# Pack attention and SwiGLU on one core: where the score products of later attentions stand in the matmul order

## The chip, the cores and the metric

The kernel runs on one core of a Trainium2 chip. TensorE multiplies (its matmuls are the rows PE, its weight loads PEld), VectorE (DVE) and ScalarE (ACT) work on what it leaves in PSUM, GpSimd (POOL) and SyncE (SP) do memsets and transfers. The metric is the device time of one execution in microseconds; the median of three runs before is 758.79 us.

## What is computed

Eight batches, each with eight heads, 576 tokens and 64 dimensions, go through two attentions, and the result goes through a gated feed-forward network:

```python
def _attn_ref(q, k, v, p):
    p_packed = sm_attn(p, k, v)              # 32 packed queries against 576 keys
    return sm_attn(q, p_packed, p_packed)    # 576 queries against the 32 packed rows

def _moe_ref(x, w_gate, w_val, w_out):       # x: 4608 x 512, d_ff 1536
    g = x @ w_gate
    silu = g * (1.0 / (1.0 + np.exp(-g)))
    val = x @ w_val
    return silu * val @ w_out
```

## The kernel before

**One batch at a time.** The kernel never forms the attention's output. For each batch b it multiplies the packed rows with the gate and value weights (the product M), and the attention weights a2 of the second attention then multiply M. M and a2 are split into a high and a low part (mh and ml, a2h and a2l), and three products of the parts stand for one in full precision.

**The steady loop.** Batches 1 to 7 run through a loop over twelve chunks fc of 128 hidden columns. In each chunk PE makes gate and value of the first 256 tokens ("A", 12 matmuls of 256 columns, `gv_chunk` with is_b False), then the output products of the previous chunk's A part (6 matmuls of 512 columns, `outs`, `out_mm`), then gate and value of the remaining 320 tokens ("B", 12 matmuls of 320 columns), then the output products of the previous chunk's B part. Chunk 0 has no output products, since there is no previous chunk: A of chunk 0, B of chunk 0 and A of chunk 1 follow each other without a gap. In the odd chunks M of the next pair of chunks follows A (`m_part`, 8 tiled matmuls of 512 columns on 64x32 tiles); in chunk 11 it is the first M of the next batch. After odd batches the leftover tokens of two batches follow as one more block of output products (p4) before the next batch starts.

**PSUM.** There are eight banks: four accumulators (acc), two for gate and value (gv), two for everything else (aux). A uses both gv banks, and so does B: gate goes to the first, value to the second. ACT reads the first (silu into sg), DVE multiplies the second with sg (hf), ACT rounds hf to hh, and DVE makes hl, the rest. A chunk's gate can start only when ACT has read the previous gate from the first bank, its value only when DVE has read the previous value from the second.

**The attention of the next batch** (d = b + 1) is put between these matmuls. For d of 2 and more its steps are: scores of the packed queries (`q_scores`, two groups of 16 tiled matmuls of 144 columns, each followed on DVE by two maxima and two subtractions, L335 and L336), exponentials on ACT, sums, a gather through DRAM of maxima and sums, the factors, a scaling and a transposing of the weights, the packing product (`q_pack`, L395, 80 small matmuls of 32 columns), and its transpose ppt. Then come the scores of the second attention (`s2_mm`, two blocks of 8 tiled matmuls of 288 columns, moved to SBUF by transposes, L421), maximum, exponential, sum, scale (L459), transpose back (L468) and split.

**What sets the order.** PE follows the program's order as it is written. In the steady loop a generator, `aux_of`, is advanced at the 4th and 8th call of `fill` in chunks 1 to 11, which are the places behind the output products of A and of B. Exponentials on ACT wait in a list, `late`, and the next `gv_chunk` takes one from it directly after its silu (L551). DVE and ACT instructions of the attention are pinned to this order (`pin`); the lows ml of M on DVE (L487, `m_lows`) are issued inside `m_part`. Each change between silu and exp on ACT is an ACT_TABLE_LOAD.

Of the kernel before, what the change touches and what calls it, by code (L numbers as in the profile page):

```python
# [59 lines left out]
def tile_pack_attention_swiglu(ctx: ExitStack, tc: tile.TileContext, qT, kT, v, vq, pT, wgv, wout, out):  # L60
# [30 lines left out]
    def pin(ins):  # L91

        return tc.keep_in_program_order(ins) if steady[0] else ins

    late = []

# [214 lines left out]

    def q_scores(b):


        k_t, p_t = kps[b]
        e = pool.tile([P, NPAR, NHP, NKQ * NP], F32, tag="s2", bufs=1, name="e1")
        z = pool.tile([P, 2, NPAR, NHP], F32, tag="z1", bufs=2, name="z1")
        sq[b] = (e, z)
        nc.gpsimd.memset(e[:, :, :, SQ:], 0.0)
        for g in range(2):  # L320
            pss = [ps(), ps()]
            for i in range(2):
                for j in range(NJ):
                    for par in range(NPAR):
                        r = slice(64 * par, 64 * par + 64)
                        nc.tensor.matmul(  # L326
                            pss[par][NP * j : NP * j + NP, i * SQ : (i + 1) * SQ],
                            p_t[r, 2 * g + i, :],
                            k_t[r, j // 2, 2 * g + i, j % 2 * SQ : j % 2 * SQ + SQ],
                            start=True, stop=True,  # L330
                        )
            hs = slice(2 * g, 2 * g + 2)
            for par in range(NPAR):
                x, m = pss[par][:, : 2 * SQ].rearrange("p (h n) -> p h n", h=2), z[:, 0, par, hs]
                pin(nc.vector.tensor_reduce(m, x, axis=AX.X, op=ALU.max))  # L335
                pin(nc.vector.tensor_tensor(  # L336
                    e[:, par, hs, :SQ], x, m.unsqueeze(2).broadcast_to([P, 2, SQ]), op=ALU.subtract
                ))
            late.append(lambda hs=hs: pin(nc.scalar.activation(e[:, :, hs, :SQ], e[:, :, hs, :SQ], AF.Exp, scale=SCALE)))
            yield  # L340
            if g == 0:
                yield

    def q_weights(b):


        e, z = sq[b]
        for g in range(2):
            if g:
                yield  # L350
            hs = slice(2 * g, 2 * g + 2)
            pin(nc.vector.tensor_reduce(z[:, 1, :, hs], e[:, :, hs, :SQ], axis=AX.X, op=ALU.add))
        zv = z.rearrange("p s r h -> p s (r h)")
        x = pool.tile([P, NJ, 2, H], F32, tag="x1", bufs=1, name="x1")
        zd = dram.tile([P, 2, H], F32, tag="zd", bufs=2, name="zd")
        nc.sync.dma_start(zd, zv)
        for i in range(NJ):
            nc.sync.dma_start(x[NP * i : NP * i + NP], zd.rearrange("(j n) s h -> n j s h", j=NJ))
        for _ in range(2):
            yield  # L360
        y = pool.tile([P, 3, NJ + 1, H], F32, tag="pp", bufs=1, name="y1")
        m, t, f = y[:, 2, 0], y[:, 2, 1], y[:, 2, 2]
# [4 lines left out]
        pin(nc.vector.tensor_tensor(y[:, 0, NJ], zv[:, 0], m, op=ALU.subtract))  # L367
        late.append(lambda: pin(nc.scalar.activation(y[:, 0], y[:, 0], AF.Exp, scale=SCALE)))
        yield
# [5 lines left out]
        yield  # L375
        a1 = pool.tile([P, NPAR, NHP, NKQ, NP], F32, tag="a1", bufs=1, name="a1")
        for par in range(NPAR):
            w = e[:, par, :, :SQ]
            pin(nc.vector.tensor_tensor(
                w, w, f[:, NHP * par : NHP * par + NHP].unsqueeze(2).broadcast_to([P, NHP, SQ]), op=ALU.mult  # L380
            ))
            pin(nc.vector.transpose(
                a1[:, par].rearrange("p h k n -> p (h k n)"), e[:, par].rearrange("p h n -> p (h n)")
            ))
            yield
        sq[b] = a1

    def q_pack(b):
        a1, v_t = sq.pop(b), vs.pop(b)
        p_p = ps()  # L390
        for hp in range(NHP):
            for k in range(NKQ):
                for g in range(P // NP):
                    par, ds = g // 2, slice(g % 2 * NP, g % 2 * NP + NP)
                    nc.tensor.matmul(  # L395
                        p_p[NP * g : NP * g + NP, NP * hp : NP * hp + NP],
                        a1[:, par, hp, k, :], v_t[:, par, hp, k, ds],
                        start=(k == 0), stop=(k == NKQ - 1),
                    )
        ppts[b] = pool.tile([P, P], F32, tag="ppt", bufs=2, name="ppt")  # L400
        pin(nc.vector.transpose(ppts[b], p_p[:, :P]))

# [19 lines left out]

    def s2_scores(b):
        for c in range(2):
            s2_mm(b, c)
            s2_block(b, c)
            yield

# [88 lines left out]
    def m_part(b, k, fcs):  # L517
        m_mm(b, k, fcs)
        m_high(b, k, fcs)
        m_lows()  # L520

# [7 lines left out]

    def gv_chunk(b, fc, is_b, fill):  # L530
        odd = b % 2
# [46 lines left out]

    def aux_of(b):

        d = b + 1
        if d == B:
            return
        yield from q_scores(d)
        yield from q_weights(d)
        if d + 1 < B:
            load_k(d + 1)
        q_pack(d)
        yield
        yield  # L590
        if d < B - 1:
            load_v(d + 1)
        s2_tiles(d)
        yield from s2_scores(d)
        if d < B - 1:
            load_q(d + 1)
        s2_a2(d)
        order = (1, 0) if d % 2 else (0, 1)
        halves = [slice(c, c + 1) for c in order]
        first, second = halves  # L600
        s2_max(d, first)
        late.append(lambda: s2_exp(d, first))
        yield
        s2_sums(d, first)
        yield
        s2_max(d, second)
        late.append(lambda: s2_exp(d, second))
        yield
        s2_scale(d, first)
        low = s2_back(d, first.start)  # L610
        yield
        low()
        s2_sums(d, second)
        yield
        s2_scale(d, second)
        low = s2_back(d, second.start)
        yield
        low()

    with tc.manual_schedule(engines={mybir.EngineType.PE}):  # L620
# [186 lines left out]
        for b in range(1, B):  # L807
            rows, accs = begin(b)
            aux = aux_of(b)
            ha, hb = {}, {}  # L810
# [7 lines left out]
            for fc in range(NFC):  # L818
                count = [0]

                def fill():
                    count[0] += 1
                    if count[0] == 2:
                        if fc == NFC - 1 and b + 1 < B:
                            run_all(aux)
# [6 lines left out]
                    if fc and count[0] in (4, 8):  # L832
                        next(aux, None)
# [4 lines left out]
                hb[fc] = gv_chunk(b, fc, True, fill)  # L838
                if fc:
                    outs(fc - 1, 1, fill)  # L840
            run_all(aux)
            outs(NFC - 1, 0, lambda: None)
# [48 lines left out]
```

## Time and profile before

| | before |
|---|---|
| median of three runs | 758.79 us (757.84 to 760.37) |
| the profiled execution | 760.24 us, of which its span is 758.5 us |
| PE busy | 745.1 us, 98% of the span |
| DVE, ACT busy | 456.6 us and 369.6 us |
| M in the steady loop | L201, 64x512, 736 rows, mean 601 ns, run on several tiles at once |
| packed-score matmuls | L326, 384 rows, mean 289 ns |
| packing product | L395, 960 rows, mean 198 ns |
| table loads on ACT | 1283 ns each |

A matmul in full precision shows as two rows. A row's length is longer than its turn on the array, since the next matmul starts before it has ended; the turn is read from start to start.

### The profile page before, as it was taken

To read this page: it belongs to the slowest core of one execution; us is meant where nothing else is said; L and a number is where in the kernel's file an instruction comes from. 1 tells how busy PE (TensorE), PEld (TensorE's weight loads), DVE (VectorE), ACT (ScalarE), POOL (GpSimd) and SP (SyncE) were. 2 spreads that over 40 slices of the span, in tenths; PEclk is the share of its full clock that TensorE was granted. 3 is DMA by queue.
4 is the path that set the end of the run, shared out by engine and by line. 5 is a ranking of instruction groups with operands and counts; after the bars stand their busy time and mean duration, and the time that the engine had idled before them with its cause. 6 is when DMAs were issued, how large, how long until landed. Compare 5 with 4: busy or idle time off the path is not lost.

```text
span 758.5 us, 15106 instructions
## 1 busy us (share of the span) xinstructions
PE 745.1 (98%) x6280; PEld 590.6 (78%) x6280; DVE 456.6 (60%) x1004; ACT 369.6 (49%) x662; POOL 2.0 (0%) x13
## 2 busy tenths in 40 slices
PE   7999999999999999998999999999999999999998
PEld 5756666787888878787788887878788787888886
DVE  5997977665756547454674556656475554743334
ACT  3777654653626436452443545464272642633331
POOL 0000000000000000000000000000000000000000
PEclk9999999999999999999999999999999999999999
DMA  9686582203011030122201221100101000010001
GB/s 355 242 319 249 207 313 78 67 3 133 1 70 67 4 134 1 56 69 71 64 29 42 69 72 63 43 15 3 71 2 69 2 3 2 1 56 1 1 1 70
DMA packets 20004, 59.15 MB, mean 78 GB/s; under 512 B 5984, under 2 KB 7008, under 8 KB 17376
## 3 DMA queue, kind: packets, MB, share of 16 engines
q1 hardware_dynamic: 19792, 58.12, 21.2%
q8 instruction: 49, 0.80, 0.4%
q14 instruction: 19, 0.16, 0.1%
q10 hardware_dynamic: 144, 0.07, 0.0%
HBM read 48.69 MB, written 9.49 MB: 77 GB/s over the span
## 4 chain that ended last, share of the span: by engine, by line
PE 95%; DVE 2%; ACT 1%; issue 1%; ACTq 0%
PE gv L544 36%; PE acc L564 30%; PE aux L201 8%; PE gv L721 6%; PE acc L747 5%; PE aux L564 4%; PE aux L395 1%; PE aux L326 1%; DVE ml L487 1%; PE acc L625 1%; PE warm_ps L625 1%; ACT mh L513 1%; PE gv_aux L201 0%; PE aux L277 0%; DVE w L133 0%
## 5 line engine op out<-in xcount | busy, mean ns | idle before, releaser
L551 ACT ACTIVATE sg<-gv 128x256 f32<-128x256 f32 (+1 forms) x168 | 68.9, 410 | 179.7 <-PE gv L544 145.4
L544 PE MATMUL gv<-a2h,ml 128*128 128x256 f32 (+1 forms) x672 | 148.4, 302 | 0.7
L544 PE MATMUL gv<-a2h,mh 128*128 128x256 f32 (+1 forms) x672 | 144.7, 297 | 0.4 <-issue 0.4
L544 PE MATMUL gv<-a2l,mh 128*128 128x256 f32 (+1 forms) x672 | 144.4, 296 | 0.0
L556 DVE TENSOR_TENSOR hf<-gv,sg 128x256 f32<-128x256 f32 x168 | 70.7, 421 | 120.6 <-PE gv L544 101.2
L564 PE MATMUL acc<-wo_h,hl 128*128 128x512 f32 x336 | 136.8, 407 | 0.0
L564 PE MATMUL acc<-wo_l,hh 128*128 128x512 f32 x336 | 132.4, 394 | 0.0
L564 PE MATMUL acc<-wo_h,hh 128*128 128x512 f32 x336 | 131.7, 392 | 0.0
L544 PEld LDWEIGHTS gv<-a2h,ml 128*128 128x128 f32 x672 | 113.9, 189 | 21.7 <-issue 7.6
L107 ACT CAST hh<-hf 128x256 fp32r<-128x256 f32 x168 | 67.9, 404 | 120.5 <-DVE hf L556 120.4
L113 DVE TENSOR_TENSOR hl<-hf,hh 128x256 fp32r<-128x256 f32 x168 | 71.0, 423 | 80.3 <-ACT hh L107 79.8
L544 PEld LDWEIGHTS gv<-a2h,mh 128*128 128x128 f32 x672 | 109.0, 191 | 0.6 <-issue 0.6
L544 PEld LDWEIGHTS gv<-a2l,mh 128*128 128x128 f32 x672 | 108.5, 190 | 0.0
L564 PEld LDWEIGHTS acc<-wo_h,hl 128*128 128x128 f32 x336 | 63.4, 189 | 42.5 <-issue 34.4
L564 PEld LDWEIGHTS acc<-wo_h,hh 128*128 128x128 f32 x336 | 63.3, 188 | 14.6
L564 PEld LDWEIGHTS acc<-wo_l,hh 128*128 128x128 f32 x336 | 63.4, 189 | 7.7
L487 DVE TENSOR_TENSOR ml<-aux,mh 128x512 fp32r<-128x512 f32 x92 | 59.0, 683 | 6.4 <-ACT mh L513 6.3
L201 PE MATMUL aux<-w,ppt 64*32 64x512 f32 (+1 forms) x784 | 52.4, 588 | 0.5 <-ACT mh L513 0.5
L513 ACT CAST mh<-aux 128x512 fp32r<-128x512 f32 x92 | 49.2, 588 | 3.6 <-PE aux L201 0.7
L747 PE MATMUL acc<-wo_f,h 128*128 128x512 f32 x96 | 44.2, 594 | 0.0
L551 ACT ACT_TABLE_LOAD x30 | 38.5, 1283 | 4.2 <-issue 3.6
L747 PEld LDWEIGHTS acc<-wo_f,h 128*128 128x128 f32 x96 | 17.3, 189 | 17.2 <-issue 15.7
(145 smaller groups left out, 756.0 us busy)
## 6 DMA issues: line engine op xcount, KB each, us to landing
st<-in_wgv SPq DMA_DIRECT2D x12, 1024.0 KB, 6.9
k_t<-in_kT SPq DMA_DIRECT2D x16, 576.0 KB, 4.9
q_t<-in_qT SPq DMA_DIRECT2D x16, 576.0 KB, 5.0
out<-ot SPq DMA_DIRECT2D x36, 256.0 KB, 2.1
v_t<-in_vq SPq DMA_DIRECT2D x6, 1280.0 KB, 5.7
st<-in_wout SPq DMA_DIRECT2D x6, 1024.0 KB, 7.2
v_t<-in_v SPq DMA_DIRECT2D x2, 1024.0 KB, 8.3
p_t<-in_pT SPq DMA_DIRECT2D x7, 64.0 KB, 2.5
```

Source lines behind the costliest of these rows:

```text
L107: e.copy(dst, src)
L113: lo.tensor_tensor(dst_l, src, dst_h.bitcast(F32), op=ALU.subtract)
L201: nc.tensor.matmul(outs[par][32 * hp : 32 * hp + 32], lhs(r, hp), rhs(r, hp), start=True, stop=True)
L487: nc.vector.tensor_tensor(*lows.pop(0), op=ALU.subtract)
L513: nc.scalar.copy(m[0][at], src)
L544: nc.tensor.matmul(pg[:, :n], m_[:, g, f, s * P : (s + 1) * P], a_[:, g, off : off + n], start=(i == 0), stop=(i == 5),)
L551: nc.scalar.activation(sg[:, :n], pgs[0][:, :n], AF.Silu)
L556: nc.vector.tensor_tensor(hf, pgs[1][:, o : o + 256], sg[:, o : o + 256], op=ALU.mult)
L564: nc.tensor.matmul(acc[:, :], h_[:, c : c + P], w_[fc // 2][:, fc % 2], start=(fc == 0 and i == 0), stop=(fc == NFC - 1 and i == 2),)
L625: nc.tensor.matmul(at[:, :P], ident, ident, start=True, stop=True)
L721: nc.tensor.matmul(held[i][s][:, :n], m_[:, g, f, s * P : (s + 1) * P], a_[:, g, off : off + n], start=(j == 0), stop=(j == len(todo) - 1),)
L747: nc.tensor.matmul(accs[2 * is_b + c], half(i)[:, c * P : c * P + P], wos[fc // 2][:, fc % 2], start=(fc == 0), stop=(fc == NFC - 1),)
```

## The change

The generator is gone. A table, `plan_of(b)`, names for each chunk and place which steps run there. The places are "a" (on ACT directly behind the silu of A), "m" (behind A, and behind M where there is one), 4 and 8 as before, and "b". The first packed scores of d move from chunk 1 of batch d - 1 to the place "m" of chunk 11 of batch d - 2 (for d = 2: to place 4 of chunk 0), the second to "m" of chunk 1, the two blocks of the second attention's scores to "m" of chunks 7 and 9. All of these but the first of d = 2 take the two gv banks in place of the aux banks. The packing product is made in two halves, at places 4 and 8 of chunk 6. The first exponential stands at "a" of chunk 0 (for d = 2 of chunk 1), the others at "a" of chunks 2, 4, 8 and 10. The lows of M are pinned, and are issued behind the steps of place "m".

```diff
-    def q_scores(b):
+    def gv_ps():
+        return ps_gv.tile([P, 512], F32, tag="gv", name="gv_aux")
+
+    def q_scores(b, g, bank=ps):
...
-            pss = [ps(), ps()]
+        pss = [bank(), bank()]
...
-    def q_pack(b):
-        a1, v_t = sq.pop(b), vs.pop(b)
-        p_p = ps()
-        for hp in range(NHP):
+    def q_pack(b, half):
+
+        if half == 0:
+            sq[b].append(ps())
+        a1, p_p = sq[b][4:]
+        v_t = vs[b]
+        for hp in range(2 * half, 2 * half + 2):
...
-    def s2_mm(b, c):
-        two[b, c] = [ps(), ps()]
+    def s2_mm(b, c, bank=ps):
+        two[b, c] = [bank(), bank()]
...
-            nc.vector.tensor_tensor(*lows.pop(0), op=ALU.subtract)
+            pin(nc.vector.tensor_tensor(*lows.pop(0), op=ALU.subtract))
...
-        if late:
-            late.pop(0)()
+        behind()
...
+                at(0, "a", lambda: q_exp(d, 0))
+            at(1, "m", lambda: q_scores(d, 1, gv_ps))
...
+            at(6, 4, lambda: q_pack(d, 0))
+            at(6, 8, lambda: q_pack(d, 1))
...
+            at(8, 8, lambda: s2_sums(d, cs), lambda: s2_scale(d, cs), lambda: s2_turn(d, c), lambda: s2_high(d, c))
+            at(9, "m", lambda: s2_mm(d, c2, gv_ps), lambda: s2_block(d, c2))
...
+            at(10, 8, lambda: s2_sums(d, cs2), lambda: s2_scale(d, cs2), lambda: s2_turn(d, c2))
...
+            at(11, "m", lambda: q_scores(d + 1, 0, gv_ps))
...
-                ha[fc] = gv_chunk(b, fc, False, fill)
+                ha[fc] = gv_chunk(b, fc, False, fill, lambda: run(fc, "a"))
+                run(fc, "m")
+                m_lows()
```

In the rows below, the first operand behind the arrow is the moving data. On PE in chunk 1 of a batch before the change (aux<-w,ppt is M, acc the output products, aux<-k_t,p_t the packed scores, gv with 320 columns is B):

```order
L544 MATMUL gv<-a2h,mh 128x256 x2
L201 MATMUL aux<-w_82,ppt 32x512 x8
L564 MATMUL acc<-wo_h,hl 128x512
L564 MATMUL acc<-wo_l,hh 128x512
L564 MATMUL acc<-wo_h,hh 128x512
L564 MATMUL acc<-wo_h,hl 128x512
L564 MATMUL acc<-wo_l,hh 128x512
L564 MATMUL acc<-wo_h,hh 128x512
L326 MATMUL aux<-k_t,p_t 32x144 x16
L544 MATMUL gv<-a2h,ml 128x320 x2
```

The same place after the change:

```order
L552 MATMUL gv<-a2h,mh 128x256 x2
L199 MATMUL aux<-w_82,ppt 32x512 x8
L328 MATMUL gv_aux<-k_t,p_t 32x144 x16
L571 MATMUL acc<-wo_h,hl 128x512
L571 MATMUL acc<-wo_l,hh 128x512
L571 MATMUL acc<-wo_h,hh 128x512
L571 MATMUL acc<-wo_h,hl 128x512
L571 MATMUL acc<-wo_l,hh 128x512
L571 MATMUL acc<-wo_h,hh 128x512
L552 MATMUL gv<-a2h,ml 128x320 x2
```

The scores have moved ahead of the six output products, directly behind M, and write the gv banks that B needs next.

On ACT at the start of a batch that follows a p4 block, before the change (sg of 256 is the silu of A, sg of 320 that of B, ot the last output copies of the previous batch):

```order
L107 COPY ot<-acc 128x512 x2
L551 ACTIVATE sg<-gv 128x256
L107 CAST hh<-hf 128x256
L551 ACTIVATE sg<-gv 128x320
L107 CAST hh<-hf 128x256
```

And after the change:

```order
L105 COPY ot<-acc 128x512 x2
L559 ACTIVATE sg<-gv 128x256
L344 ACT_TABLE_LOAD
L344 ACTIVATE e_4250<-e_4250 128x2x2x144
L105 CAST hh<-hf 128x256
L559 ACT_TABLE_LOAD
L559 ACTIVATE sg<-gv 128x320
L105 CAST hh<-hf 128x256
```

Between the silu of A and the silu of B in chunk 0 there are now a table load, an exponential and a second table load.

On DVE in chunks 10 and 11 after the change (hf of A11, the end of the second attention's scaling, its transpose back into t_4211, then the packed scores of a later attention, and the lows of M):

```order
L462 TENSOR_REDUCE r_3939<-s_3938 128x18
L563 TENSOR_TENSOR hf<-gv,sg 128x256
L463 TENSOR_SCALAR r_3939<-r_3939 128x18
L464 RECIPROCAL r_3939<-r_3939 128x18
L468 TENSOR_TENSOR s_3938<-s_3938,r_3939 128x576
L111 TENSOR_TENSOR hl<-hf,hh 128x256
L477 STREAM_TRANSPOSE t_4211<-s_3938 128x576
L337 TENSOR_REDUCE z_4251<-gv_aux 128x2
L338 TENSOR_TENSOR e_4250<-gv_aux,z_4251 128x2x144
L496 TENSOR_TENSOR ml<-aux,mh 128x512 x2
```

The reading of the score banks (L337 and L338, each there twice) stands behind the scaling and the transpose; in chunk 9 the two block transposes of the second scores stand at the same place behind the same instructions.

## Rows read from the trace of the kernel before

**Rows 1.** The page: busy time of each engine with its share of the span, and the chain of work that ended last, by engine.

```profile
PE 745.1 (98%) x6280; PEld 590.6 (78%) x6280; DVE 456.6 (60%) x1004; ACT 369.6 (49%) x662; POOL 2.0 (0%) x13
...
PE 95%; DVE 2%; ACT 1%; issue 1%; ACTq 0%
```

**Rows 2.** The timeline of PE in chunk 7 of batch 4 (start and length in us, engine, line, operation, tile, shape, and how many matmuls one row stands for): the end of A, M, the last output products, the two blocks of second-attention scores (L201 with q_t), and what follows each.

```profile
452.08 0.40 PE L544 MATMUL gv<-a2l,mh 128*128 128x256 f32 x2
...
452.32 0.40 PE L544 MATMUL gv<-a2h,mh 128*128 128x256 f32 x2
...
453.67 0.50 PE L564 MATMUL acc<-wo_h,hl 128*128 128x512 f32 x1
...
454.70 0.39 PE L564 MATMUL acc<-wo_l,hh 128*128 128x512 f32 x1
...
454.93 0.40 PE L564 MATMUL acc<-wo_h,hh 128*128 128x512 f32 x1
...
456.43 0.56 PE L544 MATMUL gv<-a2h,ml 128*128 128x320 f32 x2
...
459.45 0.40 PE L564 MATMUL acc<-wo_h,hh 128*128 128x512 f32 x1
...
459.78 0.72 PE L201 MATMUL aux<-q_t,ppt 64*32 64x288 f32 x16
...
460.43 0.50 PE L544 MATMUL gv<-a2h,ml 128*128 128x256 f32 x2
```

**Rows 3.** The waits: engine, line and tile that waited, what released it, us in total, times, longest.

```profile
PEld aux L201 <- DVE ml L487: 4.6, 12, 0.4
PEld aux L326 <- DVE ml L487: 4.6, 12, 0.4
```

**Rows 4.** The timeline of PE around the packing product: the three rows of the one in batch 4, and the last row of the one in batch 3 (the bracket is the idle time before the row).

```profile
446.07 0.39 PE L564 MATMUL acc<-wo_h,hh 128*128 128x512 f32 x1
...
446.38 1.56 PE L395 MATMUL aux<-v_t,a 128*32 128x32 f32 x160
...
447.88 0.56 PE L544 MATMUL gv<-a2h,ml 128*128 128x320 f32 x2
```

```profile
352.64 0.33 PE L395 MATMUL aux<-v_t,a 128*32 128x32 f32 x15 [2.01 <-issue]
```

**Rows 5.** Busy time in the stretch behind that row: length, then busy us of PE, PEld, DVE, ACT and POOL with their instructions, granted clock of PE (1.00 is full), DMA share, GB/s.

```profile
353.00:360.00 7.00, 7.00 (x46) 5.88 (x46) 1.72 (x5) 1.40 (x4) 0.00 (x0) 0.76 0.54 190
```

**Rows 6.** The timeline at the start of batch 4 (behind a p4 block) and of batch 3 (without one): silu of A0, start of A1, M behind A1, and the output copy on ACT.

```profile
405.15 0.38 ACT L551 ACTIVATE sg<-gv 128x256 f32<-128x256 f32 x1 [6.80 <-DVE ot L109]
...
407.45 0.40 PE L544 MATMUL gv<-a2h,ml 128*128 128x256 f32 x2
...
409.30 1.09 PE L201 MATMUL aux<-w,ppt 64*32 64x512 f32 x16
```

```profile
307.97 0.38 ACT L551 ACTIVATE sg<-gv 128x256 f32<-128x256 f32 x1 [1.54 <-PE gv L544]
...
308.66 0.59 ACT L107 COPY ot<-acc 128x512 f32<-128x512 f32 x1 [0.31 <-DMA out<-ot]
...
310.27 0.40 PE L544 MATMUL gv<-a2h,ml 128*128 128x256 f32 x2
...
312.12 1.09 PE L201 MATMUL aux<-w,ppt 64*32 64x512 f32 x16
```

**Rows 7.** The timeline of ACT where it changes to exp and back between two silus, in chunks 9 and 10 of batch 4.

```profile
471.66 0.44 ACT L551 ACTIVATE sg<-gv 128x320 f32<-128x320 f32 x1 [0.68 <-PE gv L544]
472.11 1.28 ACT L446 ACT_TABLE_LOAD   x1
473.41 0.69 ACT L446 ACTIVATE s<-s 128x576 f32<-128x576 f32 x1
474.00 0.39 ACT L107 CAST hh<-hf 128x256 fp32r<-128x256 f32 x1
474.61 1.28 ACT L551 ACT_TABLE_LOAD   x1 [0.23 <-issue]
475.91 0.38 ACT L551 ACTIVATE sg<-gv 128x256 f32<-128x256 f32 x1
```

**Rows 8.** The timeline: DVE's hf of A1 and the first output product behind M in batch 4; DVE in chunks 10 and 11 of that batch (hf, scale, transpose back, hl); the block transposes of chunk 7; a maximum and a subtraction of the packed scores.

```profile
409.48 0.42 DVE L556 TENSOR_TENSOR hf<-gv,sg 128x256 f32<-128x256 f32 x1 [0.43 <-PE gv L544]
...
410.32 0.50 PE L564 MATMUL acc<-wo_h,hl 128*128 128x512 f32 x1
```

```profile
479.04 0.41 DVE L556 TENSOR_TENSOR hf<-gv,sg 128x256 f32<-128x256 f32 x1
...
480.27 0.75 DVE L459 TENSOR_TENSOR s<-s,r 128x576 f32<-128x576 f32 x1
...
481.67 0.77 DVE L468 STREAM_TRANSPOSE t<-s 128x576 f32<-128x576 f32 x1
482.36 0.38 DVE L113 TENSOR_TENSOR hl<-hf,hh 128x256 fp32r<-128x256 f32 x1
```

```profile
460.59 0.85 DVE L421 STREAM_TRANSPOSE s<-aux 128x288 f32<-128x288 f32 x2 [0.70 <-PE aux L201]
```

```profile
413.24 0.46 DVE L335 TENSOR_REDUCE z<-aux 128x2 f32<-128x288 f32 x1 [0.85 <-PE aux L326]
...
413.73 0.46 DVE L336 TENSOR_TENSOR e<-aux,z 128x288 f32<-128x288 f32 x1
```

More of the change, by code (lines that the diff above doesn't have):

```diff
@@ L344, in q_weights @@
-    def q_weights(b):
-        e, z = sq[b]
[L348 to L353, printed above, removed]
+        if g == 0:
+            e = pool.tile([P, NPAR, NHP, NKQ * NP], F32, tag="s2", bufs=1, name="e1")
+            z = pool.tile([P, 2, NPAR, NHP], F32, tag="z1", bufs=2, name="z1")
+            sq[b] = [e, z]
+            nc.gpsimd.memset(e[:, :, :, SQ:], 0.0)
@@ new lines, in q_scores @@
+        e, z = sq[b]
+        pss = [bank(), bank()]
+        for i in range(2):
+            for j in range(NJ):
+                for par in range(NPAR):
+                    r = slice(64 * par, 64 * par + 64)
+                    nc.tensor.matmul(
+                        pss[par][NP * j : NP * j + NP, i * SQ : (i + 1) * SQ],
+                        p_t[r, 2 * g + i, :],
+                        k_t[r, j // 2, 2 * g + i, j % 2 * SQ : j % 2 * SQ + SQ],
+                        start=True, stop=True,
+                    )
@@ new lines, in q_scores, with q_exp @@
+        hs = slice(2 * g, 2 * g + 2)
+        for par in range(NPAR):
+            x, m = pss[par][:, : 2 * SQ].rearrange("p (h n) -> p h n", h=2), z[:, 0, par, hs]
+            pin(nc.vector.tensor_reduce(m, x, axis=AX.X, op=ALU.max))
+            pin(nc.vector.tensor_tensor(
+                e[:, par, hs, :SQ], x, m.unsqueeze(2).broadcast_to([P, 2, SQ]), op=ALU.subtract
+            ))
+    def q_exp(b, g):
+        x = sq[b][0][:, :, 2 * g : 2 * g + 2, :SQ]
+        pin(nc.scalar.activation(x, x, AF.Exp, scale=SCALE))
@@ L374, in q_weights, with q_turn @@
         pin(nc.vector.tensor_tensor(f, t, y[:, 0, NJ], op=ALU.mult))
[L375 to L386, printed above, removed]
-    def q_pack(b):
-        a1, v_t = sq.pop(b), vs.pop(b)
-        p_p = ps()
-        for hp in range(NHP):
+    def q_turn(b, par):
+        e, f = sq[b][0], sq[b][3][:, 2, 2]
+        if par == 0:
+            sq[b].append(pool.tile([P, NPAR, NHP, NKQ, NP], F32, tag="a1", bufs=1, name="a1"))
+        w = e[:, par, :, :SQ]
+        pin(nc.vector.tensor_tensor(
+            w, w, f[:, NHP * par : NHP * par + NHP].unsqueeze(2).broadcast_to([P, NHP, SQ]), op=ALU.mult
+        ))
+        pin(nc.vector.transpose(
+            sq[b][4][:, par].rearrange("p h k n -> p (h k n)"), e[:, par].rearrange("p h n -> p (h n)")
+        ))
+    def q_pack(b, half):
[4 more added lines that the diff above has]
+        for hp in range(2 * half, 2 * half + 2):
             for k in range(NKQ):
@@ L399, in q_pack @@
                     )
-        ppts[b] = pool.tile([P, P], F32, tag="ppt", bufs=2, name="ppt")
-        pin(nc.vector.transpose(ppts[b], p_p[:, :P]))
+        if half:
+            ppts[b] = pool.tile([P, P], F32, tag="ppt", bufs=2, name="ppt")
+            pin(nc.vector.transpose(ppts[b], p_p[:, :P]))
+            del sq[b], vs[b]
     def s2_tiles(b):
@@ L528, in h_split, with gv_chunk @@
         return hh, hl
-    def gv_chunk(b, fc, is_b, fill):
+    def gv_chunk(b, fc, is_b, fill, behind):
         odd = b % 2
@@ L808, in tile_pack_attention_swiglu @@
             rows, accs = begin(b)
-            aux = aux_of(b)
+            run = plan_of(b)
             ha, hb = {}, {}
@@ L823, in fill @@
                     if count[0] == 2:
+                        run(fc, 2)
                         if fc == NFC - 1 and b + 1 < B:
-                            run_all(aux)
                             m_part(b + 1, 0, both)
@@ L831, in fill @@
                         wout_low(fc + 5)
-                    if fc and count[0] in (4, 8):
-                        next(aux, None)
-                ha[fc] = gv_chunk(b, fc, False, fill)
+                    if count[0] in (4, 8):
+                        run(fc, count[0])
+                ha[fc] = gv_chunk(b, fc, False, fill, lambda: run(fc, "a"))
+                run(fc, "m")
+                m_lows()
                 if fc:
                     outs(fc - 1, 0, fill)
-                hb[fc] = gv_chunk(b, fc, True, fill)
+                hb[fc] = gv_chunk(b, fc, True, fill, lambda: run(fc, "b"))
                 if fc:
                     outs(fc - 1, 1, fill)
-            run_all(aux)
             outs(NFC - 1, 0, lambda: None)
```

132 lines of the change are left out of this document (54 added, 78 removed).

## The prediction

> **What bounds the kernel now.** I read the page's busy times and its chain first: PE is busy for 98% of the span and holds 95% of the chain [rows 1]. So the span is the sum of PE's turns, and an edit is worth what it adds to or takes from that sum. The other engines matter where PE has to wait for a bank. Then I read PE's timeline from start to start around the tiled matmuls [rows 2]. Third came the waits, for what stops PE there [rows 3], fourth the packing product [rows 4, 5], and last ACT and DVE at the places to which the table moves work [rows 6 to 8].
>
> **Part 1: scores directly behind M.** The turn of a gate matmul of 256 columns is 0.12 us (a pair from 452.08 to 452.32), that of an output matmul 0.23 us (454.70 to 454.93). A visit to the tiled array lasts from the end of the last full-width turn to the start of the next full-width matmul [rows 2]:
> - M: 452.56 to 453.67, 1.11 us for 512 columns.
> - First score block: 455.16 to 456.43, 1.27 us for 288 columns.
> - Second score block: 459.68 to 460.43, 0.75 us for 288 columns.
>
> The first block costs 0.52 more than the second because the lows of M still hold the aux banks. The waits say the same for both kinds of scores: 12 waits, 4.6 us each kind, about 0.4 us a wait [rows 3]. M against the second block gives (1.11 - 0.75) / 224 = 1.6 ns a column, so 288 columns are 0.46 us and the other 0.29 us is going into the tiled array and coming back. The packed scores put the same 288 columns on each tile and have the same two waits, so I give them the same prices.
>
> Directly behind M the array is already tiled, and the gv banks don't wait for the lows. A block then costs its columns, 0.48 us with a little for the start. A first block saves 1.27 - 0.48 = 0.79, a second 0.75 - 0.48 = 0.27. Two of each make 2.12 us an attention, for attentions 3 to 7. In attention 2 the first packed scores keep a visit of their own and lose only the wait (0.52), which makes 1.85. Sum: 5 x 2.12 + 1.85 = **-12.4**. If entering and leaving were not saved at all, only the waits would go: 12 x 0.52 = -6.2.
>
> **Part 2: packing in two halves.** One product takes 446.30 to 447.88, 1.58 us [rows 4]. A second entering and leaving costs 0.29 by the nearest rows [rows 2]: 6 x 0.29 = **+1.7** (bounds 0, if the halves fill gaps, and 3.4, if this tile shape costs double).
> In batch 3 the product stopped for 2.01 us with 15 matmuls left, waiting for nothing that the profile shows [rows 4], and the next 7 us ran at a mean granted clock of 0.76 [rows 5], a mean of the two levels, so about half of them at 1.2 GHz: 7 x 0.24 = 1.7 us more. Only this dense run of 160 short matmuls and their loads stops so. Half as long, with six output and twelve gate matmuls around it, I take it not to stop: -2.0 - 1.7 = **-3.7** (other end: 0).
>
> **Part 3: the first exponential at the start of a batch.** In chunk 0 A0, B0 and A1 follow each other with no output products between, and A1 needs the gate bank that the silu of B0 reads. From 6 rows on ACT: silu, load, exponential, cast, load, silu take 471.66 to 476.29, 4.63 us, of which 0.23 is idle, so 4.40 [rows 7]. The change puts this chain between the two silus of chunk 0.
> - Behind p4 (attentions 3, 5, 7): silu of A0 at 405.15, chain end 409.55, A1 0.1 later at 409.65 in place of 407.45, which is 2.2 late. A1 to M now takes 1.85 where twelve turns and 0.1 make 1.55, a 0.3 wait for hf that will be over by then. Loss 1.9 each [rows 6].
> - Without p4 (attentions 4 and 6): silu at 307.97, one output copy (0.5 to 0.59) now falls inside the chain, end 312.9, A1 at 313.0 in place of 310.27: 2.75 late, less 0.3, so 2.45 [rows 6].
>
> Sum 3 x 1.9 + 2 x 2.45 = **+10.6**. Nothing covers it: PE's order has only these matmuls there. What queues behind the chain on ACT (hh of A0, silu and hh of B0) is late by the same time, and PE needs only the bank.
> The Trainium skill, page "ScalarE: Activation LUTs", section "What ACT_TABLE_LOAD costs", adds a drain of about 1380 ns to each load of 1283 ns. The trace disagrees: the load starts at 472.11 and the exponential runs at 473.41, 1.30 later [rows 7]. By the page two drains more would stand at each of five batch starts, an estimated 13.8 us.
>
> **Part 4: gv banks held by DVE.** B's gate now waits until DVE has read the first score bank. In batch 4 hf of A starts 0.18 after M's first row; without a stall B starts 410.32 - 409.30 + 0.48 + 6 x 0.23 = 2.9 after that row [rows 6, 8].
> In chunks 9 and 11 DVE has the sums of the previous block ahead, which delay hf by some 0.1, and then scale, hl and transpose back before it reads scores. By rows: hf to scale and the scale itself 479.04 to 481.02, with the small reciprocals and one hl, 1.98; transpose to next 0.69 (481.67 to 482.36). That is 2.67, so reading starts at 0.18 + 0.1 + 2.67 = 2.95 [rows 8].
> - Chunk 9: a block transpose of about 0.46 (two take 0.85) frees the first bank at 3.4: B is 0.5 late, 6 x 0.5 = **+3.0**.
> - Chunk 11: maximum and subtraction take 0.49 + 0.46 and free it at 3.9: 1.0 late, 5 x 1.0 = **+5.0** [rows 8].
>
> In chunks 1 and 7 DVE has no scale and transpose there, reading starts once hl is out, and B waits for nothing. The lows come after, 1.2 us later than now, before the next chunk needs ml. Bounds: 0 if DVE gets there in time, 16 if both were twice as late.
> In attention 2 the first scores use both aux banks just before M of chunk 1. The four DVE instructions (1.8 us, behind hl of B0) free the second bank about 1.5 us after M wants it: **+1.5**, once (bounds 0 and 2).
>
> **Sum.** -12.4 + 1.7 - 3.7 + 10.6 + 3.0 + 5.0 + 1.5 = +5.7. The stalls of part 3 are as long as the one behind which the clock fell to 1.2 GHz [rows 4, 5], at 1.7 us a fall. That one followed a run of small matmuls, these stand among dense ones, so of five I count one: +1.7, together +7.4. Against the profiled execution that is 760.24 + 7.4 = 767.6; its 760.24 is 1.45 above the median of the runs and inside their spread, so on the median I predict 758.8 + 7.4 = **766.2**. Transfers move too (k, v and q of later attentions are issued chunks apart from now, on the same queue), always chunks ahead of their use; I cost that at nothing.
>
> **Rivals.**
> - *The waits are covered* (the other side). If the silu of B0 and DVE's reading are not what A1 and B wait for, parts 3 and 4 fall away: 758.8 - 12.4 + 1.7 - 3.7 = 744. It decides at 0.6 us a batch start and place. For it: DVE is busy for only 60% and ACT for 49% [rows 1]. Against it: both are in order, and the chain of 4.4 us stands in 1.8 us of B0. Chance 0.09. If only part 4 is covered, 766.2 - 8 = 758, no change to slightly faster: 0.15.
> - *The clock falls at every batch start.* Four falls more, 6.8 us: 773. For it: one row of such a stall. Chance 0.12.
> - *Leaving M's mode isn't saved*, so the change takes only the waits away: 6.2 more, 772. For it: the moving data and the weights differ from M's. Against: all are 64x32 tiles [rows 2]. Chance 0.08.
> - *Every table load drains*, from the page named above: with its estimate, 766.2 + 13.8 = 780. The row of 1.30 speaks against it. Chance 0.02.
> - The forecast: 0.54.
>
> **Chances.** What this measurement can tell from no change is about 0.3%, 2.3 us, so faster means below 756.5 and slower above 761.1. Faster is the first rival and a third of the second case: 0.14. No change is most of the rest of that case and a little of the forecast's low end: 0.13. Slower: 0.73. The forecast's own range is 761 to 770; to leave out no more than 2 in 10 I take 755 to 774.
>
> **What would show it.** Right: score rows starting within 0.1 us of M's end, no row of PE waiting for the lows; PE idle about 2.2 us before A1 in chunk 0 of batches 2 to 6, released by ACT's silu; 0.5 and 1.0 us before B in chunks 9 and 11, released by DVE. Wrong: A1 of chunk 0 starting where it does now, B in chunk 11 without a wait, or scores behind M taking 0.75 us or more.

## The result and the profile after

The changed kernel takes 767.4 us (median of 13 runs, 761.95 to 769.1), the kernel before on the same chip 760.37 (13 runs, 757.84 to 760.99). The ratio is 1.0088, with a 95% interval from 1.0068 to 1.0108: slower, where 766.2 was predicted. The profiled execution took 768.19, with a span of 766.1; that is 7.95 above the 760.24 of before; between the medians the change is 7.0. One spread is wide: the runs at a mean granted clock of 0.998 took 761.95 and 762.29, those at 0.984 and 0.986 took 769.1 and 769.0.

The busy times and the chain on the page after, beside [rows 1]:

```profile
PE 742.3 (97%) x6280; PEld 598.4 (78%) x6280; DVE 454.2 (59%) x1004; ACT 372.7 (49%) x662; POOL 2.0 (0%) x13
...
PE 80%; DVE 9%; ACT 8%; DMA 1%; issue 1%; SPq 0%; ACTq 0%; DVEq 0%
```

PE is busy for 2.8 us less, and the span is 7.6 longer. DVE and ACT hold 17% of the chain, where they held 3% before. That share doesn't measure the loss: a kernel further down that takes 15 us less than this one (e1) has 16%. The waits after (columns as in [rows 3]) name the places:

```profile
PE gv L552 <- ACT sg L559: 11.1, 5, 2.5
...
PEld gv L552 <- DVE s L436: 3.2, 6, 0.7
PE gv L552 <- DVE e L338: 2.9, 5, 0.6
```

The two waits for DVE's ml of [rows 3], 9.2 us together, are gone. In their place are five waits of PE for a silu, 11.1 us by this view, and five for the subtraction of the packed scores, 2.9 us. Six weight loads wait for the block transposes (0.5 each); the matmuls behind them are late by less.

PE's timeline in chunks 6 and 7 of batch 4 (columns as in [rows 2]): the second half of the packing product, and M with a score block directly behind it.

```profile
454.39 0.90 PE L408 MATMUL aux<-v_t,a 128*32 128x32 f32 x80
455.22 0.50 PE L552 MATMUL gv<-a2h,ml 128*128 128x256 f32 x2
455.56 0.40 PE L552 MATMUL gv<-a2l,mh 128*128 128x256 f32 x2
455.80 0.40 PE L552 MATMUL gv<-a2h,mh 128*128 128x256 f32 x2
...
456.52 0.40 PE L552 MATMUL gv<-a2h,mh 128*128 128x256 f32 x2
456.85 1.09 PE L199 MATMUL aux<-w,ppt 64*32 64x512 f32 x16
457.73 0.69 PE L199 MATMUL gv_aux<-q_t,ppt 64*32 64x288 f32 x16
458.35 0.50 PE L571 MATMUL acc<-wo_h,hl 128*128 128x512 f32 x1
```

The last pair of A is through its turns at 456.76, and the first output product starts at 458.35: 1.59 for M and a block, where M alone took 1.11 [rows 2]. So a block of q_t costs 0.48. Behind a half of the packing product there is a second cost that is easily overlooked. The pair at 455.22 holds PE for 0.34, the next for 0.24. The first full-width row after a visit to the tiled array is some 0.1 us longer than its turns, in the kernel before as well.

The start of batch 4 on ACT and PE, beside [rows 6]:

```profile
407.28 0.39 ACT L559 ACTIVATE sg<-gv 128x256 f32<-128x256 f32 x1 [6.61 <-DVE ot L107]
407.69 1.28 ACT L344 ACT_TABLE_LOAD   x1
408.98 0.69 ACT L344 ACTIVATE e<-e 128x576 f32<-128x576 f32 x1
...
409.98 1.28 ACT L559 ACT_TABLE_LOAD   x1
411.27 0.44 ACT L559 ACTIVATE sg<-gv 128x320 f32<-128x320 f32 x1
```

```profile
409.29 0.46 PE L552 MATMUL gv<-a2h,mh 128*128 128x320 f32 x2
411.76 0.79 PE L552 MATMUL gv<-a2h,ml 128*128 128x256 f32 x2 [2.02 <-ACT sg L559]
412.35 0.63 PE L552 MATMUL gv<-a2l,mh 128*128 128x256 f32 x2
412.78 0.63 PE L552 MATMUL gv<-a2h,mh 128*128 128x256 f32 x2
...
416.39 0.50 PE L571 MATMUL acc<-wo_h,hl 128*128 128x512 f32 x1
```

The chain on ACT ends at 411.7, 4.43 us after the silu of A0 began, as the 4.40 of [rows 7] had it. B0's last pair of turns (0.29) is over at 409.58, and A1 starts at 411.76, so it is 2.18 late; the bracket counts from the end of the last row and has 2.02. In batches 3 and 5 it is 2.67 and 2.66 late. Then each pair of A1 takes 0.43 in place of 0.24. The windows of 3 us behind the five waits (columns as in [rows 5]) say what that is:

```profile
229.00:232.00 3.00, 3.00 (x55) 1.71 (x54) 0.85 (x2) 1.18 (x3) 0.00 (x0) 0.71 0.00 0
317.00:320.00 3.00, 3.00 (x44) 1.73 (x47) 0.85 (x3) 0.79 (x2) 0.00 (x0) 0.58 0.02 5
413.00:416.00 3.00, 3.00 (x47) 2.04 (x52) 0.80 (x3) 0.79 (x2) 0.00 (x0) 0.65 0.00 0
502.00:505.00 3.00, 3.00 (x53) 1.60 (x53) 0.91 (x3) 0.98 (x4) 0.00 (x0) 0.70 0.00 0
597.00:600.00 3.00, 3.00 (x59) 2.10 (x58) 1.77 (x5) 1.83 (x5) 0.00 (x0) 1.00 0.03 8
```

Each of the first four windows lies partly at 1.2 GHz, the fifth wholly at 2.4. From the start of A1 to the first output product it takes 4.63 us in batch 4 (411.76 to 416.39) and 3.20 in batch 6 (596.17 to 599.37), so this fall cost 1.43. The same two rows give 1.50, 1.52 and 1.51 in batches 2, 3 and 5: 6.0 us for the four.

DVE and PE in chunk 11 of batch 4, the place of the wait for e:

```profile
485.49 0.76 DVE L468 TENSOR_TENSOR s<-s,r 128x576 f32<-128x576 f32 x1
...
486.50 0.77 DVE L477 STREAM_TRANSPOSE t<-s 128x576 f32<-128x576 f32 x1
487.20 0.42 DVE L337 TENSOR_REDUCE z<-gv_aux 128x2 f32<-128x288 f32 x1
487.65 0.46 DVE L338 TENSOR_TENSOR e<-gv_aux,z 128x288 f32<-128x288 f32 x1
```

```profile
488.25 0.53 PE L552 MATMUL gv<-a2h,ml 128*128 128x320 f32 x2 [0.58 <-DVE e L338]
```

DVE reads the first bank from 487.20 on, behind the scaling and the transpose, and B starts when the subtraction is out: 0.73 behind the end of the output products. In chunk 9, where a block transpose frees the bank, B was 0.23 or 0.24 late (0.43 in the last batch).

### The profile page after: what moved, and what is told of

It is laid out like the page before. It is cut to its first block, busy times and chain, and to the rows that moved or that the text cites. A ratio compares the mean times of both kernels' runs of the same rounds, so it can differ in the third digit from the quotient of the medians.

```text
span 766.1 us, 15139 instructions
## 1 busy us (share of the span) xinstructions
PE 742.3 (97%) x6280; PEld 598.4 (78%) x6280; DVE 454.2 (59%) x1004; ACT 372.7 (49%) x662; POOL 2.0 (0%) x13
## 4 chain that ended last, share of the span: by engine, by line
PE 80%; DVE 9%; ACT 8%; DMA 1%; issue 1%; SPq 0%; ACTq 0%; DVEq 0%
PE gv L552 30%; PE acc L571 25%; PE gv L738 6%; PE aux L199 6%; PE acc L764 5%; PE aux L571 4%; ACT L559 3%; DVE hf L563 2%; DVE hl L111 1%; ACT hh L105 1%; DMA v_t<-in_v 1%; PE aux L408 1%; DVE s L468 1%; ACT sg L559 1%; ACT L455 1%
## 5 line engine op out<-in xcount | busy, mean ns | idle before, releaser
L552 PE MATMUL gv<-a2h,ml 128*128 128x256 f32 (+1 forms) x672 | 148.8, 303 | 14.7 <-ACT sg L559 11.1
L552 PEld LDWEIGHTS gv<-a2h,ml 128*128 128x128 f32 x672 | 115.4, 191 | 33.2 <-ACT sg L559 12.4
L199 PE MATMUL aux<-w,ppt 64*32 64x512 f32 (+1 forms) x784 | 54.9, 605 | 0.7 <-ACT mh L522 0.5
L764 PEld LDWEIGHTS acc<-wo_f,h 128*128 128x128 f32 x96 | 17.3, 189 | 17.2 <-issue 16.5
```

The source lines that it names most:

```text
L199: nc.tensor.matmul(outs[par][32 * hp : 32 * hp + 32], lhs(r, hp), rhs(r, hp), start=True, stop=True)
L552: nc.tensor.matmul(pg[:, :n], m_[:, g, f, s * P : (s + 1) * P], a_[:, g, off : off + n], start=(i == 0), stop=(i == 5),)
L764: nc.tensor.matmul(accs[2 * is_b + c], half(i)[:, c * P : c * P + P], wos[fc // 2][:, fc % 2], start=(fc == 0), stop=(fc == NFC - 1),)
```

## The experiments

Three theories for the loss stood against each other: (A) the table loads of the first exponential, put between the two silus of chunk 0; (B) the clock falls behind those waits; (C) the gate banks that DVE holds in chunks 9 and 11. Beside them there was one question of gain: what the scores behind M are worth by themselves. All of it was tried on the changed kernel unless said otherwise, with the kernel before run on the same chip; the ratios are to that. The kernel before took 760.37 beside the result and 759.22 to 759.69 beside the runs below, so a difference between the 767.4 of the result and a run below is uncertain by about 1 us.

**The first exponential in chunk 1 (e1).** Only the place of that step changes.

```diff
-                at(1, "a", lambda: q_exp(d, 0))
-            else:
-                at(0, "a", lambda: q_exp(d, 0))
+            at(1, "a", lambda: q_exp(d, 0))
```

> The changed kernel with the first exponential of attentions 3 to 7 moved from place a of chunk 0 to place a of chunk 1 (where attention 2 already has it); nothing else. Theory (the chain load, exp, cast, load between the two silus of chunk 0 holds back A1, and the long idle time lets the clock fall): the five waits of 2.2 and 2.7 us before A1 of chunk 0 and the low-clock stretches behind them go, 10 to 11 us and some 6 us: 751, between 749 and 754, faster than the kernel before, and no wait of PE on ACT in chunk 0. Rival (the cost sits in the scores behind M and DVE's late reading in chunks 9 and 11, and the exponential only shows it): the wait moves to chunk 1 and the time stays within 3 us of 767.

Measured: 752.5 (751.73 to 753.06), ratio 0.9909 [0.9891, 0.9927]. PE at the start of batch 4:

```profile
401.81 0.46 PE L552 MATMUL gv<-a2h,mh 128*128 128x320 f32 x2
402.10 0.40 PE L552 MATMUL gv<-a2h,ml 128*128 128x256 f32 x2
402.34 0.40 PE L552 MATMUL gv<-a2l,mh 128*128 128x256 f32 x2
402.58 0.40 PE L552 MATMUL gv<-a2h,mh 128*128 128x256 f32 x2
403.07 0.47 PE L552 MATMUL gv<-a2h,ml 128*128 128x256 f32 x2
403.39 0.40 PE L552 MATMUL gv<-a2l,mh 128*128 128x256 f32 x2
...
406.77 0.40 PE L571 MATMUL acc<-wo_h,hh 128*128 128x512 f32 x1
407.27 0.53 PE L552 MATMUL gv<-a2h,ml 128*128 128x320 f32 x2
```

The gate half of A1 starts where B0's turns end (402.10), and its pairs take 0.24 again. The value half (403.07) is 0.25 late, as it was in the kernel before (408.42 behind 407.93 in batch 4). A small price shows at the new place: B of chunk 1 is 0.27 late. So this one step of the table was worth 14.9 us (767.4 - 752.5), or 13.7 when each is taken against its own runs of the kernel before (+7.0 and -6.7): more than the whole loss either way.

**No table loads (e2).** The first exponential becomes a silu, which needs no other table. This changes the weights of the first attention; the time of the step is the same 0.69.

```diff
-        pin(nc.scalar.activation(x, x, AF.Exp, scale=SCALE))
+        pin(nc.scalar.activation(x, x, AF.Silu if b > NEARLY and g == 0 else AF.Exp, scale=SCALE))
```

> The changed kernel with the first exponential of attentions 3 to 7 replaced by a silu of the same data at the same place, so that ACT needs no table load in chunk 0; this changes the weights of the first attention. Theory (the two table loads, 2.6 us of the 4.4 us chain, are what A1 waits for; the 0.69 us instruction alone fits beside B0): 751 to 753, with no wait over 0.3 us before A1. Rival (an extra ACT instruction between the silus is already too much, loads or not): the wait shrinks by 2.6 us at most where it was 2.7 and to 0 where it was 2.2, but if ACT's queue is late for another reason it stays near 2 us and the time near 765.

Measured: 750.14 (749.96 to 751.07), ratio 0.9882 [0.9861, 0.9903]. The exponential's own 0.69 still stands between the two silus, and PE no longer waits for them; the time is 0.9 under the expected range. The two loads of 1.28 are what made A1 late.

**PE kept busy in the wait (e3).** Matmuls of 128 columns are put between B0 and A1, their result unread; the wait for the silu stays.

```diff
+                at(0, 4, lambda: warm_up(9, ps()))
```

> The changed kernel with nine matmuls of 128 columns on the identity (some 2.1 us) put between B0 and A1 of chunk 0 in batches 2 to 6; their result is used nowhere. Theory (behind four of the five waits the clock falls because PE idles, and a fall costs about 1.5 us): PE has work in the wait, the waits before A1 stay as late as they are, the granted clock stays at 1.00 behind them, and the time is 761 to 763. Rival (the clock falls for another reason, or a fall costs nothing since PE waits anyway): 766 to 769 as the changed kernel, or more if the matmuls delay A1.

Measured: 760.81 (760.13 to 761.97, 10 runs), ratio 1.0021 [1.0012, 1.0031]. PE in batch 3, and the window behind it:

```profile
311.20 2.17 PE L643 MATMUL aux<-ident 128*128 128x128 f32 x18
313.86 0.50 PE L552 MATMUL gv<-a2h,ml 128*128 128x256 f32 x2 [0.49 <-ACT sg L559]
314.20 0.40 PE L552 MATMUL gv<-a2l,mh 128*128 128x256 f32 x2
```

```profile
314.00:318.00 4.00, 4.00 (x64) 3.06 (x65) 2.49 (x7) 2.27 (x5) 0.00 (x0) 1.00 0.00 0
```

A1 is as late as before this edit (2.66 behind B0's turns, which end at 311.20), but at full clock. Without saving any wait, the filling gave back 6.6 us (767.4 - 760.81), or 5.4 when each is taken against its own runs of the kernel before; the rows of the four falls added up to 6.0. That is theory B, parted from A.

**The packing product whole again (e4).** Both halves at place 4 of chunk 6.

```diff
-            at(6, 8, lambda: q_pack(d, 1))
+            at(6, 4, lambda: q_pack(d, 1))
```

> The changed kernel with both halves of the packing product at place 4 of chunk 6, one behind the other as in the kernel before. Theory (two halves cost 0.25 to 0.35 us more each attention than one product, and prevent a stop of PE for 2 us with a fall of the clock behind it, which the kernel before shows in one product of six): 1.5 to 2 us less by the visits, and 3.7 us more for each product that stops; with one stop about 769, with none 765.5. Rival (the stop is no matter of the product's length): no stop, 765 to 766.

Measured: 765.45 (764.16 to 767.2), ratio 1.0081 [1.0059, 1.0104], against 1.0088 [1.0068, 1.0108] for the changed kernel: too close to part the two. A stop is back in one batch, now the second, 1.03 long, and the clock stayed at full speed behind it (1.00 from 267 to 274), so the 3.7 a stop of the expectation doesn't hold. It doesn't stand in the packing product but among the gate matmuls of B, 1 us behind it:

```profile
263.20 1.56 PE L408 MATMUL aux<-v_t,a 128*32 128x32 f32 x160
264.69 0.56 PE L552 MATMUL gv<-a2h,ml 128*128 128x320 f32 x2
...
266.72 0.41 PE L552 MATMUL gv<-a2h,mh 128*128 128x320 f32 x1 [1.03 <-issue]
```

The kernel before has a stop of 0.37 at that place too, in its second batch (266.81). The five waits at the batch starts are there as in the changed kernel (2.01 or 2.5 us), and three of them ended in a clock fall: from the start of A1 to the first output product it takes 3.18 us in batches 2 and 3 and 4.69 to 4.73 in the others.

**Before, with the halves alone (e6).** In the kernel before, the packing product gets a second place.

```diff
         for hp in range(NHP):
+            if hp == 2:
+                yield
...
-        q_pack(d)
-        yield
+        yield from q_pack(d)
```

> The kernel before with only the packing product in two halves, at places 4 and 8 of chunk 6. Theory (two halves cost 0.3 us an attention more, and take away one stop of 2.0 us with the fall of the clock behind it, 3.7 us in the profiled execution, and the 0.9 us wait of the first product): -2.7, so 756 to 758. Rival (the stop is not in most executions, or it moves elsewhere): +1 to +2, 760 to 761.

Measured: 758.74 (757.7 to 760.43, 11 runs) beside 759.69, ratio 0.9988 [0.9977, 0.9999]. That lies between the two expectations. No stop is left, as part 2 took it, and what the halves cost is a little less than what the stops cost: about 0.9 us, the interval just short of no change.

**Own visits for the scores (e5).** On e1, all four blocks go back to the aux banks and to visits of their own, at places 4; the exponentials, sums and factors of the first attention go back with them to places near those that they had before the change (not shown in the cut).

```diff
-            at(1, "m", lambda: q_scores(d, 1, gv_ps))
+            at(1, 4, lambda: q_scores(d, 0))
+            at(2, 4, lambda: q_scores(d, 1))
...
-            at(7, "m", lambda: s2_mm(d, c, gv_ps), lambda: s2_block(d, c))
+            at(7, 4, lambda: s2_mm(d, c), lambda: s2_block(d, c))
...
-            at(9, "m", lambda: s2_mm(d, c2, gv_ps), lambda: s2_block(d, c2))
+            at(9, 4, lambda: s2_mm(d, c2), lambda: s2_block(d, c2))
...
-            at(11, "m", lambda: q_scores(d + 1, 0, gv_ps))
```

> The kernel of e1 with all four score blocks of an attention taken back to visits of their own, in the aux banks, at places 4 of chunks 1, 2, 7 and 9 (the exponentials and sums of the first attention follow at the places where they stood before the change); the halves of the packing product and the table stay. Theory (the scores behind M are worth what the prediction's part 1 says, and cost the waits of part 4): an attention pays 1.28 + 0.74 + 2 x 1.27 in place of 4 x 0.48 to 0.54, some 2.6 to 2.9 us more with what each leaving costs, 16 to 17 us in all; it gets back the waits of 0.24 in chunk 9 and 0.73 in chunk 11, 5 us, and 1.3 of attention 2: 752.5 + 9 = 761, between 759 and 763. Rival (e1 is faster than the kernel before for another reason, by packing halves or by the order of DVE and ACT, and the visits are hidden): within 2 us of 752.5.

Measured: 768.54 (768.04 to 769.14), ratio 1.0122 [1.0107, 1.0136], a miss. In three of the visits the blocks took what [rows 2] give (1.28, 0.74, 1.27). The fourth, in chunk 9, took 2.18:

```profile
471.23 0.40 PE L571 MATMUL acc<-wo_h,hh 128*128 128x512 f32 x1
472.40 1.31 PE L199 MATMUL aux<-q_t,ppt 64*32 64x288 f32 x16 [0.77 <-DVE ml L496]
473.64 0.56 PE L552 MATMUL gv<-a2h,ml 128*128 128x320 f32 x2
```

The lows of M, which free the aux banks, stand on DVE behind the scale and the transpose there (ml at 471.69). So own visits need DVE too, in another order. The terms of the expectation add up to 762.7 (752.5 + 16.5 - 5 - 1.3) and not to the 761 written there; the fourth visit is 0.91 longer than a visit of 1.27 in five batches and 1.24 longer in the last, 5.8 in all, and that makes 768.5.

**The scale of s2 ahead of the highs (e7).** On e1, the sums and the scale of the second attention move from place 8 to place "b" of chunks 8 and 10, directly behind the silu of B. On DVE they then run ahead of hf of B of the same chunk.

```diff
-            at(8, 8, lambda: s2_sums(d, cs), lambda: s2_scale(d, cs), lambda: s2_turn(d, c), lambda: s2_high(d, c))
+            at(8, "b", lambda: s2_sums(d, cs), lambda: s2_scale(d, cs))
+            at(8, 8, lambda: s2_turn(d, c), lambda: s2_high(d, c))
...
-            at(10, 8, lambda: s2_sums(d, cs2), lambda: s2_scale(d, cs2), lambda: s2_turn(d, c2))
+            at(10, "b", lambda: s2_sums(d, cs2), lambda: s2_scale(d, cs2))
+            at(10, 8, lambda: s2_turn(d, c2))
```

> The kernel of e1 with the sums and the scaling of the second attention's blocks issued ahead of DVE's hf of B in chunks 8 and 10, and only the transpose back left behind it. Theory (B of chunks 9 and 11 waits because sums, scale and transpose stand before the reading of the score banks on DVE): DVE reaches the banks 1.4 us earlier in chunks 9 and 11, the waits of 0.73 and 0.23 go, 5 to 6 us: 747 to 748. Rival (the wait moves into hf of B, since the scaling now stands before it, and value of the next A waits for its bank): 751 to 753.

Measured: 749.26 (748.47 to 749.93), ratio 0.9867 [0.9852, 0.9882], between the two expectations. Of the waits of the gate banks the view now has one of DVE alone:

```profile
PE gv L552 <- DVE t L566: 1.3, 6, 0.2
```

```profile
458.45 0.47 PE L552 MATMUL gv<-a2h,ml 128*128 128x256 f32 x2 [0.21 <-DVE t L566]
...
462.12 0.39 PE L571 MATMUL acc<-wo_h,hh 128*128 128x512 f32 x1
462.34 0.46 PE L552 MATMUL gv<-a2h,ml 128*128 128x320 f32 x2
```

B of chunk 9 follows the output products without a wait (462.12 to 462.34), and so it does in chunk 11. The scale now holds up DVE's reading of the second bank in chunk 8 instead (hf of B, and with it t, the 64 tokens left over): the value matmuls of A9 start 0.37 late, in each of six batches, of which the bracket shows 0.21. Theory C holds for 1.6 + 3.6 = 5.2 us, and the new wait takes 2.2 back: 3.0, beside 3.2 measured.

**e7 with the whole packing product (e8).** The edit of e4 on e7.

> The kernel of e7 with the packing product whole at place 4 of chunk 6. Theory (halves cost 0.3 to 0.35 an attention and only pay where a whole product stops): 2 us less by the visits, and 1 to 3.7 us more for each product that stops, of which e4 showed one: 746 to 749 against e7. Rival (the halves pay by themselves, since instructions for so many short matmuls run out): slower than e7 by over 1 us.

Measured: 748.69 (747.59 to 749.58), ratio 0.9864 [0.9847, 0.9881]: the same as e7 within what the runs can tell. One stop of 1.05 stands at the same place of the second batch again, and no fall follows. Halving removes stops and adds visits of about the same sum.

**Own visits with the early scale (e9).** The edit of e7 on e5, which makes it the counterpart of e7 without scores behind M.

> The previous run with own visits for all four score blocks, with the sums and the scale of s2 ahead of the highs as in e7. If the 8 us that this run lay above e1 beyond the visits themselves came from the lows that stood behind the scale and the transposes (0.92 us in each of 6 batches, 5.5 us), the time is 768.5 - 5.5 = 763, within 762 to 764, and the block of chunk 9 takes 1.2 to 1.4 instead of 2.19. Then score blocks behind M are worth 749.3 - 763 = -13.7 against own visits, beside the 12.4 that part 1 gave. Rival: the scale isn't what makes the lows late (the transposes are, which stay): 767 to 769, with 2.0 or more in chunk 9.

Measured: 766.0 (765.54 to 766.81), ratio 1.0088 [1.0073, 1.0103]. The block in chunk 9:

```profile
471.68 1.31 PE L199 MATMUL aux<-q_t,ppt 64*32 64x288 f32 x16
472.92 0.56 PE L552 MATMUL gv<-a2h,ml 128*128 128x320 f32 x2
```

Its visit is 1.43 in place of 2.18, from the end of the last output turn at 471.49. So the lows behind the scale were the cause, 0.75 x 6 = 4.5. The time missed the expected 762 to 764: it left out that the value of A9 is late by 0.37 here too, 2.2 in all; 4.5 - 2.2 = 2.3, beside 2.5 measured. Between e9 and e7 lie 16.7 us: that is what scores behind M are worth here against own visits at these places, with the steps that moved along with them. The rows of the visits alone give 16.4.

**Only the early scale (e10).** The edit of e7 on the changed kernel, the first exponential still in chunk 0.

> The changed kernel, its first exponential still in chunk 0, with only the sums and the scale of s2 ahead of the highs. If the waits of chunks 9 and 11 are apart from those at the batch starts, the gain is that of e7 against e1, 3.2: 767.4 - 3.2 = 764, within 762.5 to 766, with four clock falls as before. Rival: the shorter end of chunk 11 moves the batch start so that fewer of the waits end in a clock fall (each 1.5): 760 to 762.5.

Measured: 762.52 (760.5 to 764.21), ratio 1.0047 [1.003, 1.0063]. The windows behind the waits of batches 4, 5 and 6:

```profile
405.00:409.00 4.00, 3.56 (x28) 2.60 (x36) 1.51 (x5) 1.58 (x4) 0.00 (x0) 0.63 0.00 0
493.00:497.00 4.00, 3.75 (x44) 2.32 (x52) 1.83 (x5) 1.47 (x5) 0.00 (x0) 0.73 0.00 0
588.50:592.50 4.00, 3.85 (x63) 2.96 (x64) 2.36 (x7) 2.34 (x6) 0.00 (x0) 1.00 0.02 6
```

All five waits are there (2.0 or 2.5 us), but only two of them ended in a fall in the profiled execution, which took 760.5; in batches 2 and 3 it takes 3.18 us from the start of A1 to the first output product, as without a fall. The runs spread over 3.7 us, from 760.5 at a clock of 0.995 to 764.21 at 0.991. With e3 as the measure of no falls, this kernel without falls would be 760.8 - 3.2 = 757.6, and two falls of 1.5 make 760.6. So the median stands on the border of the two expectations: the gain of the early scale, and about one fall fewer than four. What decides whether a fall follows one of these waits stays open.

## Why the prediction was right

The forecast of 766.2 was 1.2 off, and its sum of +7.4 stands against 7.95 in the profiled executions. Between the medians the change is +7.0, from a base that is 1.6 above the 758.8 of the forecast (three runs there, thirteen here). The mechanisms named were those that the runs showed, but that the sum came so close is in part luck: the parts are less good than the sum.

- **Part 1 (-12.4)** was right in its prices and left out something. Blocks behind M cost 0.48 and 0.54 where 0.48 was taken; by the rows that is 11.7. The forecast closed a visit at the start of the next full-width matmul; that row then lasts 0.1 us longer. With 23 visits fewer this is 2.3 us more of gain. The rival "leaving M's mode isn't saved" fell with these rows, since a visit without a wait took 0.75, and with e9 against e7: of the 16.7 us the waits for the lows are 10.6 by the rows of the visits.
- **Part 2 (+1.7 - 3.7)** was right. The halves take 0.91 each, 1.82 for 1.58, which with the 0.1 for leaving again makes 2.1 in six batches, and neither stop nor fall is left there. One wait had been overlooked: the first product of before waited 0.70 for its weights a, and with that its turn took 0.9 longer; the half doesn't wait. By e4, e6 and e8, each with the runs of its own set, halving gains or loses under 1 us in all. The stop is not tied to a fall (e4, e8), so the 1.7 belong to the one execution of before. Nor does only the dense run itself stop, as part 2 had it: three stops stand among the gate matmuls behind a whole product (0.37 in before, 1.03 in e4, 1.05 in e8).
- **Part 3 (+10.6)** was right in mechanism and size. A1 is 2.18 late three times and 2.67 and 2.66 in batches 3 and 5, and the 0.25 that its value half waited before is gone, as part 3 took it. From the end of B0's turns to M it takes 3.81 in batch 6, which had no fall, and 4.27 in batch 3 of e3, in place of 1.85: 1.96 and 2.42, or 10.7 in all. Removing the loads (e2) or moving the exponential (e1) removes the waits. The load takes 1.28 and the exponential starts 1.29 behind its start (407.69 to 408.98), so the drain that the Trainium skill, page "ScalarE: Activation LUTs", section "What ACT_TABLE_LOAD costs", adds is again not seen; the rival built on it is out.
- **Part 4 (+9.5)** was oversized. The chain on DVE was as described, but B is 0.23 and not 0.5 late in chunk 9 (1.6 us in all), and 0.73 and not 1.0 in chunk 11 (3.65). Two small errors added up in the step "reading starts at 0.18 + 0.1 + 2.67 = 2.95". In chunk 11 of batch 4 M begins at 484.47; reading starts 2.73 behind that. And B without its wait of 0.73 would start 3.05 behind it, not 2.9, because of the long first row behind a visit. Attention 2 cost 1.3 where 1.5 was taken: its M and first block take 2.92 in chunk 1 of batch 1, 1.65 elsewhere.
- **The clock (+1.7)** was undersized. The step that failed is "these stand among dense ones, so of five I count one": four of the five waits ended in a fall, at 1.5 each, 6.0 us. The rival "the clock falls at every batch start" was nearly what happened; its 773 was too high because it counted five falls at 1.7 and stood on a part 4 that was too large and a gain on leaving that was left out.

In the profiled executions the terms are -11.7 - 2.3 + 2.1 - 0.9 - 3.7 + 10.7 + 6.6 + 6.0 = 6.8; another 1.0 is from the first 20 us of the program, whose clock was 0.83 in place of 0.91 and which the change doesn't touch (the first gate pass starts at 23.49 in place of 22.45). That makes 7.8 against 7.95. Part 4 was 2.9 too dear, the gain on leaving and on the first product 3.2 too small, and the clock 4.3 too cheap: errors that nearly cancel.

The change holds a gain of 1.3% over the kernel before that its table gives away. With the first exponential in chunk 1 and the scale ahead of the highs it takes 749.26 (e7), faster than both kernels; with the whole packing product 748.69 (e8), which the runs can't tell from it.

## What to carry to other kernels

When work is moved off the bounding engine's path, read what else moves in the same table: here one activation with its two table loads, put where nothing else is queued for PE, cost about as much as all the score blocks gained. Price a wait of PE twice, once by its length and once by the clock behind it, and do so for every place where it occurs, since a wait among dense matmuls lowered the clock as well as one behind small ones. A bank that is taken from another engine's slack is only free if that engine's queue in front of its release is short; moving 2 us of DVE work ahead of it removed the wait and left a smaller one.

## What was not expected of the hardware

- A wait of 2.2 to 2.7 us of PE in the middle of dense work was followed by a stretch at 1.2 GHz in four of five places of one execution (after), three of five of another (e4) and two of five of a third (e10), at about 1.5 us each. Like waits (2.18 in batches 2, 4 and 6 of after) went either way, so the time of a kernel with such waits is itself spread: 761.95 to 769.1 in 13 runs, against 760.13 to 761.97 in 10 runs of the one with the waits filled (e3).
- The slow stretch can begin after PE is busy again. In batch 5 of e10 the pairs of A1 behind the wait have their usual turns, and M behind them takes 1.71 (494.88 to 496.59) where 0.88 is usual.
- Behind or in the dense run of 160 short matmuls PE stopped for 2.01 us in one batch and 0.37 in another of before, and once for 1.03 and 1.05 in e4 and e8, and no wait is shown for it. No execution with the run in halves has such a stop. Its cause stays open.
- A visit to the tiled array costs beyond its own rows: the first full-width row behind it is 0.1 us longer, whatever its tile shape was. A plain wait shows the same (403.07 to 403.39 in e1, 0.32 in place of 0.24), so it isn't shown that the tiles cause it.
